# An output product moved behind those of the next two batches, its sums kept in SBUF

## The chip, the cores and the metric

One core of a Trainium2 chip runs the whole program. The metric is the device time of one execution in microseconds, the median of several runs. The engines are TensorE (PE, with PEld for its weight loads), VectorE (DVE), ScalarE (ACT), GpSimd (POOL) and SyncE (SP); SyncE's queue issues every DMA of this kernel.

## The reference

Attention with a causal mask and a bias, then two feed-forward parts, for 4 batches of 576 tokens, 512 channels. The change lies between the last lines of the first part and the first of the second:

```python
# first part (x is the attention's output)
h = gelu(x @ w_in);  u, v = halves of h
gated = u * (einsum('ts,bsd->btd', w_sg, norm(v) * g_ln) + b_sg)
x2 = x + gated @ w_out
# second part (x is x2)
theta = x2 @ w_theta
y = einsum(w_tok_r, x2 * cos(theta)) + einsum(w_tok_i, x2 * sin(theta))
u = x2 + y
out = u + max(u @ w_ch, 0)
```

## The kernel before

All values are fp32. A matrix product is made of three: each operand is split into a high half (rounded, on ScalarE) and a low half (the rest, on VectorE or GpSimd), and high x high, high x low and low x high are summed in PSUM. Activations lie transposed, channels in the partitions, in four strips (dt or ft) of 128 channels by 576 tokens; a strip is multiplied in two halves of 288 tokens (HALF).

The attention, lines 419 to 452, runs for all batches with the first part of the earlier batches as fill. Behind it stands the last batch's first part, and with it what the change touches, in run (lines 850 to 896):

- ffn_in and ffn_gate of batch 3. ffn_gate (lines 649 to 672) writes the gated strips of every batch to memory (gd, line 672). x, the attention's output, is in memory too (xd).
- The second part's weights: second_weights (lines 914 to 934) is a generator, prep, that loads 64-bit words (wraw), and in split64 (lines 455 to 472) makes fp32 of them in three VectorE instructions (wta, lines 466, 467 and 469) and the two halves, the low one on GpSimd (wol, wtl, wkl, wcl). Such a unit is called a weight group below. Each step of the output product pulls one (self.later).
- wout (lines 675 to 700) is the output product of one batch. It loads four gated strips (gr), splits them (gh on ScalarE, gl on VectorE, line 90), and for each of four strips dt loads x (xr, line 689), multiplies 2 x 12 matmuls (wo), adds x on VectorE (line 697) and writes x2 to memory (x2d, line 699).
- theta (lines 703 to 766) is the start of the second part of one batch. It loads the batch's x2 in one transfer (x2T, line 708), splits it (x2s, with a small copy xt on GpSimd), and for each of five token tiles makes a transposition (tp), a product (th, 12 matmuls) and a chain over ScalarE and VectorE (kk, an, sn, cs) to cos and sin, and two products zf of them with x2.
- mix (lines 778 to 814) multiplies the split zf (zh, zl) with the token weights (yo, 27 matmuls for each of eight outputs), then with w_ch (co), and writes the result.

The order of wout and theta is set in run: batches 0 and 1 as fill of ffn_gate(3), batch 2 alone, batch 3 as fill of theta(0), then mix(0) with theta(1) as fill, and so on. wout of batch 0 writes x2 to memory and theta(0) reads it back. From what is written there, tile's scheduler makes each engine's own order by priorities and a timeline of its own, so a step that is moved in the code moves others too. Each engine works through its list in order and waits where an operand or a buffer is not there.

PSUM tiles are shared by tags of two banks each: yo, ex, fo, tp. wraw and xr have three buffers, gr two, gh and gl six, x2T two.

Of the kernel before, what the change touches and what calls it, by code (L numbers as in the profile page):

```python
# [9 lines left out]
F32 = mybir.dt.float32  # L10
# [8 lines left out]
B, H, S, D = 4, 8, 576, 64  # L19
DM, DFF = 512, 1024  # L20
FH = DFF // 2
P = 128
# [27 lines left out]
class Kernel:  # L50
# [621 lines left out]
            nc.sync.dma_start(self.gd[b, ft], uT[:, ft])  # L672


    def wout(self, b, pool):
        nc = self.nc
        gs = []
        for ft in range(4):
            gr = pool.tile([P, S], F32, name="gr", tag="gr")
            nc.sync.dma_start(gr, self.gd[b, ft])  # L680
            gh = pool.tile([P, S], F32R, name="gh", tag="gh", bufs=6)
            gl = pool.tile([P, S], F32R, name="gl", tag="gl", bufs=6)
            self.rnd("act", gh, gr)
            self.sub("dve", gl, gr, gh)
            gs.append((gh, gl))
        for dt in range(4):
            ds = slice(dt * P, (dt + 1) * P)
            xr = pool.tile([P, S], F32, name="xr", tag="xr", bufs=3)
            nc.sync.dma_start(xr, self.xd[b, dt])
            for a, m in HALF:  # L690
                o = self.psB.tile([P, 512], F32, name="wo", tag=self.wtag)
                for ft in range(4):
                    gh, gl = gs[ft]
                    self.mm(o[:, 0:m], self.woh[:, ft, ds], gh[:, a:a + m], ft == 0, False)
                    self.mm(o[:, 0:m], self.wol[:, ft, ds], gh[:, a:a + m], False, False)
                    self.mm(o[:, 0:m], self.woh[:, ft, ds], gl[:, a:a + m], False, ft == 3)
                nc.vector.tensor_tensor(xr[:, a:a + m], o[:, 0:m], xr[:, a:a + m], op=ALU.add)  # L697
                if a:
                    nc.sync.dma_start(self.x2d[b, dt], xr)
                yield 1480.0  # L700


    def theta(self, b):

        nc = self.nc
        x2T = self.p1.tile([P, 4, S], F32, name="x2T", tag="x2T", bufs=2)
        self.x2T[b] = x2T
        nc.sync.dma_start(x2T, self.x2d[b].rearrange("t p s -> p t s"))
        xs = []
        for dt in range(4):  # L710
            x = self.p1.tile([P, 2, S], F32R, name="x2s", tag="hl", bufs=4)
# [105 lines left out]
    def run(self):  # L817
        nc = self.nc
        with ExitStack() as root, ExitStack() as right2, ExitStack() as left2:
# [40 lines left out]
            with ExitStack() as ws:  # L860
                self.stg = self.pool(ws, "stg", side="right")
                for n, _ in enumerate(self.ffn_in(B - 1)):
                    if n % 8 == 0:
                        self.later(prep)
                f3s.close()
                wq = self.pool(ws, "wq", bufs=2, side="right")

                def wo(bs):
                    for b in bs:
                        for c in self.wout(b, wq):  # L870
                            self.later(prep)
                            yield c

                self.ftags = ("yo", "ex")
                self.fill, self.ratio = wo((0, 1)), 0.8
                for c in self.ffn_gate(B - 1):
                    self.pace(c)
                left.close()
                self.wc = self.pool(left2, "wc")
                self.p1 = self.pool(left2, "p1")  # L880
                self.drain()
                self.wtag = "ex"
                for _ in wo((2,)):
                    pass
                self.fill, self.ratio = wo((3,)), 0.5
                for c in self.theta(0):
                    self.pace(c)
                self.drain()
                for _ in prep:
                    pass  # L890
# [86 lines left out]
```

## Time and profile before

| | |
|---|---|
| median of 3 runs | 708.98 us (708.6 to 710.29) |
| the profiled execution | 710.52 us |
| its span, first to last instruction | 708.7 us |
| mean granted clock of TensorE | 0.981 of full |
| TensorE matmuls (PE) busy | 662.4 us, 93% |
| VectorE (DVE) busy | 455.4 us, 64% |
| ScalarE (ACT) busy | 371.7 us, 52% |
| GpSimd (POOL) busy | 261.3 us, 37% |
| read from and written to memory | 60.38 and 19.10 MB |

In the span the attention fills some 363 us, the first part of batch 3 the time to about 416 us, the output products with the first theta the time to 507 us, and the mixing of the four batches the rest. A matmul's recorded duration is longer than the distance to the next one, because matmuls overlap; the distance is what counts, and idle time in brackets names what ended it. The granted clock is a share of 2.4 GHz; 0.5 is the lower level.

### The profile page before, as it was taken

To read this page: it belongs to the slowest core of one execution; us is meant where nothing else is said; L and a number is where in the kernel's file an instruction comes from. 1 tells how busy PE (TensorE), PEld (TensorE's weight loads), DVE (VectorE), ACT (ScalarE), POOL (GpSimd) and SP (SyncE) were. 2 spreads that over 40 slices of the span, in tenths; PEclk is the share of its full clock that TensorE was granted. 3 is DMA by queue.
4 is the path that set the end of the run, shared out by engine and by line. 5 is a ranking of instruction groups with operands and counts; after the bars stand their busy time and mean duration, and the time that the engine had idled before them with its cause. 6 is when DMAs were issued, how large, how long until landed. Compare 5 with 4: busy or idle time off the path is not lost.

```text
span 708.7 us, 12076 instructions
## 1 busy us (share of the span) xinstructions
PE 662.4 (93%) x4288; PEld 580.9 (82%) x4288; DVE 455.4 (64%) x902; ACT 371.7 (52%) x856; POOL 261.3 (37%) x273
## 2 busy tenths in 40 slices
PE   6899789799999999999999769998999999999998
PEld 4667557588879788897879669887999989989997
DVE  5566687766438544484449998898976368368522
ACT  3566656677367743786427534673753255156100
POOL 6556564458426554375237653423000100010000
PEclk9899989999999999999999989999999999999999
DMA  4646666624423354321143778972000300300101
GB/s 131 188 142 193 203 196 182 183 78 147 125 83 109 102 154 142 103 84 44 68 143 104 243 240 297 328 255 85 34 1 25 110 1 1 134 1 1 68 1 68
DMA packets 52972, 85.02 MB, mean 120 GB/s; under 512 B 9968, under 2 KB 19600, under 8 KB 52912
## 3 DMA queue, kind: packets, MB, share of 16 engines
q1 hardware_dynamic: 52912, 84.25, 38.3%
q8 instruction: 34, 0.56, 0.3%
q14 instruction: 26, 0.21, 0.1%
HBM read 60.38 MB, written 19.10 MB: 112 GB/s over the span
## 4 chain that ended last, share of the span: by engine, by line
PE 49%; DVE 7%; DMA 4%; ACT 3%; issue 2%; POOL 0%; SPq 0%; DVEq 0%; ACTq 0%
PE yo L93 16%; PE co L93 7%; PE fo L93 7%; PE th L93 6%; PE Y L93 3%; PE wo L93 3%; PE sc L93 3%; PE T L332 2%; DVE wta L469 1%; DVE wta L467 1%; DMA x2T<-x2d 1%; PE tp L720 1%; DVE wta L466 1%; DVE gl L90 1%; DMA wraw<-in_moe_w_ch 1%
## 5 line engine op out<-in xcount | busy, mean ns | idle before, releaser
L293 ACT ACTIVATE E<-sc,negm 128x448 f32<-128x448 f32 (+4 forms) x160 | 87.0, 551 | 51.4 <-DVE negm L292 50.3
L292 DVE TENSOR_REDUCE negm<-sc 128x1 f32<-128x448 f32 (+4 forms) x160 | 73.6, 481 | 43.4 <-PE sc L93 42.2
L93 PE MATMUL yo<-wkh,zl 128*128 128x288 f32 x288 | 85.3, 297 | 0.0
L93 PE MATMUL yo<-wkh,zh 128*128 128x288 f32 x288 | 85.2, 296 | 0.0
L93 PE MATMUL yo<-wkl,zh 128*128 128x288 f32 x288 | 85.1, 296 | 0.0
L332 PE MATMUL T<-ident,E 128*128 128x128 f32 x400 | 73.4, 298 | 5.0 <-ACT E L293 3.4
L93 PE MATMUL sc<-kA,qA 128*128 128x128 f32 (+2 forms) x192 | 64.9, 359 | 9.5 <-ACT E L293 7.8
L332 PEld LDWEIGHTS T<-ident,E 128*128 128x128 f32 x400 | 58.2, 194 | 17.2 <-issue 5.7
L93 PE MATMUL sc<-kB,qB 68*128 68x128 f32 (+3 forms) x192 | 61.6, 331 | 3.4 <-DMA qB<-cpos 1.8
L93 PE MATMUL fo<-x,wih 128*128 128x288 f32 x256 | 58.4, 306 | 1.5 <-ACT vT L607 0.8
L86 POOL TENSOR_SCALAR xt<-x2s 128x128 fp32r<-128x128 f32 x16 | 9.9, 634 | 134.2 <-DVE x2s L90 134.2
L93 PEld LDWEIGHTS yo<-wkh,zh 128*128 128x128 f32 x288 | 54.1, 188 | 0.3
L93 PEld LDWEIGHTS yo<-wkl,zh 128*128 128x128 f32 x288 | 54.1, 188 | 0.2
L93 PEld LDWEIGHTS yo<-wkh,zl 128*128 128x128 f32 x288 | 53.9, 188 | 0.2
L93 PE MATMUL co<-u,wch 128*128 128x288 f32 x256 | 53.1, 295 | 0.0
L93 PEld LDWEIGHTS sc<-kA,qA 128*128 128x128 f32 x192 | 38.6, 209 | 16.3 <-ACT E L293 8.4
L90 POOL TENSOR_TENSOR kB<-K,kA 64x576 fp32r<-64x576 f32 x32 | 46.6, 1456 | 10.5 <-ACT kA L82 9.1
L93 PE MATMUL wo<-gh,woh 128*128 128x288 f32 x128 | 40.4, 319 | 9.1 <-DVE xr L697 6.4
L86 POOL TENSOR_SCALAR qA<-Q 128x576 fp32r<-128x576 f32 x32 | 22.6, 705 | 69.7 <-PE sc L93 29.9
L90 POOL TENSOR_TENSOR qA<-Q,qA 64x576 fp32r<-64x576 f32 x32 | 46.3, 1446 | 2.6
L93 PE MATMUL Y<-Ef,vr 128*64 128x512 f32 (+3 forms) x256 | 47.0, 444 | 0.0
L93 PEld LDWEIGHTS fo<-x,wih 128*128 128x128 f32 x256 | 43.3, 192 | 3.9 <-issue 1.2
(169 smaller groups left out, 1878.5 us busy)
## 6 DMA issues: line engine op xcount, KB each, us to landing
Q<-in_q SPq DMA_DIRECT2D x64, 144.0 KB
K<-in_k SPq DMA_DIRECT2D x64, 144.0 KB
qB<-qA SPq DMA_DIRECT2D x32, 144.0 KB
xT<-rd SPq DMA_DIRECT2D x32, 144.0 KB
xd<-xT SPq DMA_DIRECT2D x16, 288.0 KB
gd<-uT SPq DMA_DIRECT2D x16, 288.0 KB
gr<-gd SPq DMA_DIRECT2D x16, 288.0 KB
xr<-xd SPq DMA_DIRECT2D x16, 288.0 KB
```

Of the source, the lines that this page charges most:

```text
L86: nc.gpsimd.tensor_scalar(out, src, 1.0, 1.0, op0=ALU.mult, op1=ALU.mult)
L90: e.tensor_tensor(out, a, f32(hi), op=ALU.subtract)
L93: self.nc.tensor.matmul(out, lhsT, rhs, start=start, stop=stop)
L292: nc.vector.tensor_reduce(negm[:, c:c + 1], o, axis=ax, op=ALU.max, negate=True)
L293: nc.scalar.activation(out, o, AF.Exp, bias=negm[:, c:c + 1], accum_out=sm[:, j * 5 + c:j * 5 + c + 1])
L332: nc.tensor.transpose(T[:, col:col + P], e, self.ident)
L466: nc.vector.tensor_scalar(ta.bitcast(U32), ta.bitcast(U32), 3, None, op0=ALU.logical_shift_left)
L467: nc.vector.scalar_tensor_tensor(ta.bitcast(U32), Hi, 0x80000000, ta.bitcast(U32), op0=ALU.bitwise_and, op1=ALU.bitwise_or)
L469: nc.vector.scalar_tensor_tensor(ta.bitcast(U32), L, 29, ta.bitcast(U32), op0=ALU.logical_shift_right, op1=ALU.bitwise_or)
L720: nc.tensor.transpose(tp[0:r, dt * P:(dt + 1) * P], x2T[:, dt, a:a + r], self.ident)
```

## The change

wout gets an argument kept. With it, x is loaded straight into the batch's x2T tile (a strip dt of it in place of xr), the sums are made there, and nothing is written to memory. x2_tile makes such a tile; theta makes and loads one only where the batch has none. In run, the fill of ffn_gate(3) is wout of batches 1 and 2 in place of 0 and 1; batch 0's, with kept, stands alone behind them, where batch 2's stood; batch 3's is the fill of theta(0) as before.

```diff
--- before.py
+++ after.py
@@ -672,7 +672,8 @@
             nc.sync.dma_start(self.gd[b, ft], uT[:, ft])
 
 
-    def wout(self, b, pool):
+    def wout(self, b, pool, kept=False):
+
         nc = self.nc
         gs = []
         for ft in range(4):
@@ -685,7 +686,7 @@
             gs.append((gh, gl))
         for dt in range(4):
             ds = slice(dt * P, (dt + 1) * P)
-            xr = pool.tile([P, S], F32, name="xr", tag="xr", bufs=3)
+            xr = self.x2T[b][:, dt] if kept else pool.tile([P, S], F32, name="xr", tag="xr", bufs=3)
             nc.sync.dma_start(xr, self.xd[b, dt])
             for a, m in HALF:
                 o = self.psB.tile([P, 512], F32, name="wo", tag=self.wtag)
@@ -695,17 +696,21 @@
                     self.mm(o[:, 0:m], self.wol[:, ft, ds], gh[:, a:a + m], False, False)
                     self.mm(o[:, 0:m], self.woh[:, ft, ds], gl[:, a:a + m], False, ft == 3)
                 nc.vector.tensor_tensor(xr[:, a:a + m], o[:, 0:m], xr[:, a:a + m], op=ALU.add)
-                if a:
+                if a and not kept:
                     nc.sync.dma_start(self.x2d[b, dt], xr)
                 yield 1480.0
 
 
+    def x2_tile(self):
+        return self.p1.tile([P, 4, S], F32, name="x2T", tag="x2T", bufs=2)
+
     def theta(self, b):
 
         nc = self.nc
-        x2T = self.p1.tile([P, 4, S], F32, name="x2T", tag="x2T", bufs=2)
-        self.x2T[b] = x2T
-        nc.sync.dma_start(x2T, self.x2d[b].rearrange("t p s -> p t s"))
+        if b not in self.x2T:
+            self.x2T[b] = self.x2_tile()
+            nc.sync.dma_start(self.x2T[b], self.x2d[b].rearrange("t p s -> p t s"))
+        x2T = self.x2T[b]
         xs = []
         for dt in range(4):
             x = self.p1.tile([P, 2, S], F32R, name="x2s", tag="hl", bufs=4)
@@ -867,12 +872,12 @@
 
                 def wo(bs):
                     for b in bs:
-                        for c in self.wout(b, wq):
+                        for c in self.wout(b, wq, b in self.x2T):
                             self.later(prep)
                             yield c
 
                 self.ftags = ("yo", "ex")
-                self.fill, self.ratio = wo((0, 1)), 0.8
+                self.fill, self.ratio = wo((1, 2)), 0.8
                 for c in self.ffn_gate(B - 1):
                     self.pace(c)
                 left.close()
@@ -880,7 +885,8 @@
                 self.p1 = self.pool(left2, "p1")
                 self.drain()
                 self.wtag = "ex"
-                for _ in wo((2,)):
+                self.x2T[0] = self.x2_tile()
+                for _ in wo((0,)):
                     pass
                 self.fill, self.ratio = wo((3,)), 0.5
                 for c in self.theta(0):
```

How it moves the lists of the engines, at three places. The number behind a name tells one tile from another.

SyncE, the issues around 424 to 434 us of the trace of before. gr and xr belong to output products, xd and gd are x and the gated strips in memory, wraw are raw weights. Before:

```order
L689 DMA xr_4859<-xd_57 128x576
L699 DMA x2d_58<-xr_4683 128x576
L909 DMA wraw_4918<-in_moe2_w_tok_i 128x576
L909 DMA wraw_4985<-in_moe2_w_tok_i 128x576
L699 DMA x2d_58<-xr_4771 128x576
L689 DMA xr_4969<-xd_57 128x576
L909 DMA wraw_5009<-in_moe2_w_tok_r 128x576
L680 DMA gr_5169<-gd_59 128x576
L689 DMA xr_5018<-xd_57 128x576
L699 DMA x2d_58<-xr_4859 128x576
```

and with the change:

```order
L690 DMA xr_4859<-xd_57 128x576
L690 DMA x2T_5169<-xd_57 128x576
L700 DMA x2d_58<-xr_4683 128x576
L915 DMA wraw_4918<-in_moe2_w_tok_i 128x576
L915 DMA wraw_4985<-in_moe2_w_tok_i 128x576
L690 DMA x2T_5169<-xd_57 128x576 x3
L700 DMA x2d_58<-xr_4771 128x576
L915 DMA wraw_5009<-in_moe2_w_tok_r 128x576
L690 DMA xr_4969<-xd_57 128x576
L681 DMA gr_5170<-gd_59 128x576
```

The four loads of batch 0's x, into x2T_5169, stand ahead of the write of x2d from xr_4683, and of three loads (wraw_5009, xr_4969 and the next gr). In the order before, no such load stands here.

VectorE, the start of theta of batch 0. x2s are its split halves, wta weight groups, an and kk the chain to cos and sin; gl_5190 is the last strip of batch 2 before, and gl_5401 the first of batch 3 in the change. Before:

```order
L90 TENSOR_TENSOR x2s_5397<-x2T_5380,x2s_5397 128x576
L90 TENSOR_TENSOR gl_5190<-gr_5187,gh_5189 128x576
L466 TENSOR_SCALAR wta_5108<-wta_5108 128x288
L466 TENSOR_SCALAR wta_5134<-wta_5134 128x288
L467 SCALAR_TENSOR_TENSOR wta_5108<-wraw_5107,wta_5108 128x288
L467 SCALAR_TENSOR_TENSOR wta_5134<-wraw_5133,wta_5134 128x288
L469 SCALAR_TENSOR_TENSOR wta_5108<-wraw_5107,wta_5108 128x288
L466 TENSOR_SCALAR wta_5161<-wta_5161 128x256
L469 SCALAR_TENSOR_TENSOR wta_5134<-wraw_5133,wta_5134 128x288
L467 SCALAR_TENSOR_TENSOR wta_5161<-wraw_5160,wta_5161 128x256
L90 TENSOR_TENSOR gl_5410<-gr_5407,gh_5409 128x576
L469 SCALAR_TENSOR_TENSOR wta_5161<-wraw_5160,wta_5161 128x256
```

and with the change:

```order
L698 TENSOR_TENSOR x2T_5169<-wo_5195,x2T_5169 128x288
L698 TENSOR_TENSOR x2T_5169<-wo_5218,x2T_5169 128x288
L469 SCALAR_TENSOR_TENSOR wta_5108<-wraw_5107,wta_5108 128x288
L467 SCALAR_TENSOR_TENSOR wta_5134<-wraw_5133,wta_5134 128x288
L466 TENSOR_SCALAR wta_5161<-wta_5161 128x256
L90 TENSOR_TENSOR x2s_5373<-x2T_5169,x2s_5373 128x576
L469 SCALAR_TENSOR_TENSOR wta_5134<-wraw_5133,wta_5134 128x288
L467 SCALAR_TENSOR_TENSOR wta_5161<-wraw_5160,wta_5161 128x256
L698 TENSOR_TENSOR x2T_5169<-wo_5242,x2T_5169 128x288
L90 TENSOR_TENSOR gl_5401<-gr_5398,gh_5400 128x576
L469 SCALAR_TENSOR_TENSOR wta_5161<-wraw_5160,wta_5161 128x256
L698 TENSOR_TENSOR x2T_5169<-wo_5265,x2T_5169 128x288
```

Before, the four x2s stand together (x2s_5397 is the last), and kk follows the weight groups wta_5108 to wta_5161. With the change the sums into x2T_5169 alternate with weight groups, and each x2s follows the two sums of its strip; seven more weight groups stand between this piece and the first kk.

TensorE, the same place: wo are matmuls of the output product, tp the transpositions, th the theta product. Before:

```order
L93 MATMUL wo_5143<-gl_4966,woh_4170 128x288
L720 MATMUL tp_5402<-ident_149,x2T_5380 128x128 x4
L720 MATMUL tp_5493<-ident_149,x2T_5380 128x128 x4
L93 MATMUL wo_5195<-gh_5183,woh_4170 128x288
L93 MATMUL wo_5195<-gh_5183,wol_4171 128x288
L93 MATMUL wo_5218<-gh_5183,woh_4170 128x288
L93 MATMUL wo_5218<-gh_5183,wol_4171 128x288
L93 MATMUL wo_5195<-gl_5184,woh_4170 128x288
L93 MATMUL wo_5218<-gl_5184,woh_4170 128x288
L93 MATMUL th_5449<-wth_4172,x2s_5382 128x512
L93 MATMUL th_5449<-wtl_4173,x2s_5382 128x512
```

and with the change:

```order
L93 MATMUL wo_5265<-gh_5190,wol_4171 128x288
L93 MATMUL wo_5265<-gl_5191,woh_4170 128x288
L93 MATMUL th_5440<-wth_4172,x2s_5373 128x512
L93 MATMUL th_5440<-wtl_4173,x2s_5373 128x512
L93 MATMUL th_5491<-wth_4172,x2s_5373 128x512
L93 MATMUL th_5491<-wtl_4173,x2s_5373 128x512
L93 MATMUL th_5440<-wth_4172,x2s_5373 128x512
L93 MATMUL th_5491<-wth_4172,x2s_5373 128x512
L93 MATMUL wo_5289<-gh_5172,woh_4170 128x288
L93 MATMUL wo_5289<-gh_5172,wol_4171 128x288
```

Before, the transpositions of a whole token tile stand together, and th_5449 follows with all its strips, between matmuls of batch 2's first two output tiles. With the change theta goes strip by strip in two token tiles at once (th_5440 and th_5491), each strip behind 24 matmuls of batch 0's output product.

## Rows read from the trace of the kernel before

**Rows 1.** Busy time by stretch, core 0: us, engines with instructions, PEclk, DMA share, GB/s

```profile
418.00:426.00 8.00, 6.14 (x25) 6.14 (x26) 6.70 (x13) 2.19 (x5) 3.00 (x4) 0.57 0.78 259
426.00:436.00 10.00, 9.59 (x72) 9.36 (x71) 8.58 (x21) 4.55 (x10) 3.22 (x4) 1.00 0.80 259
432.00:451.00 19.00, 17.55 (x128) 16.60 (x127) 16.86 (x35) 10.13 (x22) 6.27 (x8) 1.00 0.96 328
451.00:470.00 19.00, 19.00 (x111) 16.79 (x110) 16.82 (x38) 12.12 (x24) 6.90 (x7) 1.00 0.94 323
...
507.30:530.00 22.70, 22.70 (x168) 22.12 (x167) 18.51 (x34) 12.03 (x23) 0.00 (x0) 1.00 0.00 1
486.00:492.00 6.00, 5.58 (x31) 5.57 (x32) 3.89 (x10) 3.82 (x7) 0.73 (x1) 0.72 0.31 98
```

**Rows 2.** What TensorE waited for, 432 to 510 us: total us, times, longest us

```profile
PE wo L93 <- DVE xr L697: 2.2, 4, 1.3
PE th L93 <- DVE x2s L90: 1.2, 2, 0.9
PE th L93 <- DVE xr L697: 0.7, 1, 0.7
```

**Rows 3.** TensorE in order of time: start us, us, count, idle before

```profile
419.86 0.61 PE L93 MATMUL wo<-gh,woh 128*128 128x288 f32 x1 [4.24 <-DVE xr L697]
...
479.87 0.47 PE L93 MATMUL th<-wth,x2s 128*128 128x512 f32 x1
...
482.12 0.39 PE L93 MATMUL th<-wtl,x2s 128*128 128x512 f32 x1
...
484.66 0.50 PE L93 MATMUL th<-wth,x2s 128*128 128x512 f32 x1 [0.94 <-DVE x2s L90]
486.42 0.40 PE L93 MATMUL wo<-gh,woh 128*128 128x288 f32 x1 [1.26 <-DVE xr L697]
```

**Rows 4.** The chain that ended last, 430 to 508 us: start us, us, what

```profile
429.89 1.21 PE wo L93 x9
...
432.62 3.83 DMA gr<-gd
...
440.07 7.89 DMA x2T<-x2d
...
504.20 0.44 PE tp L720 x4
504.64 2.77 PE th L93 x12
```

**Rows 5.** VectorE's groups by line, 432 to 492 us: count, busy us, mean ns, idle

```profile
L697 DVE TENSOR_TENSOR xr<-wo,xr 128x288 f32<-128x288 f32 x21 | 9.1, 450 | 2.1 <-PE wo L93 2.0
L469 DVE SCALAR_TENSOR_TENSOR wta<-wraw,wta 128x288 uint32<-128x288 uint32 (+1 forms) x16 | 8.0, 502 | 0.1
L90 DVE TENSOR_TENSOR gl<-gr,gh 128x576 fp32r<-128x576 f32 x10 | 7.8, 776 | 2.1 <-ACT gh L82 2.0
L467 DVE SCALAR_TENSOR_TENSOR wta<-wraw,wta 128x288 uint32<-128x288 uint32 (+1 forms) x16 | 7.1, 446 | 0.1
L90 DVE TENSOR_TENSOR x2s<-x2T,x2s 128x576 fp32r<-128x576 f32 x8 | 6.5, 840 | 0.0
L466 DVE TENSOR_SCALAR wta<-wta 128x288 uint32<-128x288 uint32 (+1 forms) x16 | 5.6, 357 | 0.5 <-ACT wta L465 0.5
...
L759 DVE TENSOR_TENSOR zf<-x,cs 128x512 f32<-128x512 f32 x4 | 2.8, 710 | 0.1
```

**Rows 6.** VectorE in order of time, at 450 and at 480 us

```profile
450.77 1.42 DVE L90 TENSOR_TENSOR x2s<-x2T,x2s 128x576 fp32r<-128x576 f32 x2
...
480.65 2.05 DVE L90 TENSOR_TENSOR x2s<-x2T,x2s 128x576 fp32r<-128x576 f32 x2
```

**Rows 7.** GpSimd in order of time, at 480 us

```profile
480.85 2.44 POOL L90 TENSOR_TENSOR wcl<-wta,wch 128x256 fp32r<-128x256 f32 x2
```

**Rows 8.** ScalarE in order of time, at 490 us

```profile
490.79 0.58 ACT L745 COPY sn<-th 64x512 f32<-64x512 f32 x1 [1.42 <-DVE zf L759]
```

## The prediction

> **What bounds the kernel now.** I read the busy times by stretch first, then the waits of TensorE, and last the rows around each wait. The change neither adds nor removes a matmul, and TensorE is busy all through the stretches around it [rows 1]. So the end moves only by what TensorE idles, or works at the lower clock. The change touches the stretch from about 420 us, behind the last gate product, to 507 us, where the mixing of the first batch begins. There the reader is to see two things. Once the mixing runs TensorE has no gap (22.70 of 22.70 us from 507 us, [rows 1]), so a microsecond saved before it is one saved at the end. And between 432 and 470 us the other resources are nearly full too: the DMA engines are at 0.96 and 0.94, VectorE is busy 16.9 of 19 and 16.8 of 19 us [rows 1].
>
> What TensorE loses after 432 us is small. Matmuls of the output product waited 2.2 us for sums (xr) of VectorE, those of theta 1.2 us for split halves (x2s) and 0.7 us for a sum [rows 2]: 4.1 us. At 479.87 to 482.12 us eight theta matmuls start 0.32 us apart in place of the 0.23 us of the chain (12 in 2.77 us) [rows 3, 4]: 0.7 us. And from 486 to 492 us the granted clock is 0.72 on average [rows 1], which costs 6 x 0.28 = 1.7 us; it fell to the lower level (1.2 GHz) after TensorE had waited 0.94 and 1.26 us within 4 us [rows 3]. Together **6.5 us**, the most that the change can win. A longer wait, before 419.86 us (4.24 us, [rows 3]), lies ahead of the first row that the change moves on TensorE and VectorE; I leave it as it is.
>
> **The change, part by part.** *Removed:* four writes of x2d and one load of x2T of 1152 KB for batch 0, so 2.3 MB less traffic, 7 us at the 328 GB/s of the stretch [rows 1]. The load took 7.89 us and is in the chain [rows 4]. But it costs TensorE little: while it was under way TensorE had 17.55 busy us in 19 [rows 1], with output products of the third batch. In its own loss the load has at most the 0.7 us wait of theta and some of the 2.2 us. The transfer is no gain by itself; what counts is which engine is late next. SyncE issues 9 - 4 = 5 transfers fewer.
>
> *Not removed:* batch 1 takes the place of batch 0. Its x2T of 1152 KB is loaded at the same place in SyncE's queue, behind the third gr of what is now batch 0, and the fourth gr is queued behind it. The DMA engines thus stay full until about 450 us. Nobody needs that x2T before theta of batch 1, near 485 us, so its own landing is covered by 40 us.
>
> *Moved forward:* the four loads of x for batch 0 (now into x2T) stand ahead of x2d, wraw, xr and gr that were next. That is 4 x 288 KB, 3.5 us at 328 GB/s; the DMA engines have a 0.2 share free in 426 to 436 us [rows 1], 2 us, so some 1.5 us of it reaches the transfers behind. They are free to start: the tile lies where the gate's operands were, and TensorE had ended the gate 4.24 us before 419.86 us [rows 3]. First to feel it is gr of the next batch: issued at 432.62 us, it took 3.83 us and stands in the chain [rows 4]. In the new order VectorE has to do both gl of that batch before the sum of strip xr_5018, where it did one before; TensorE waits for that sum, and the matmuls of wo_5195 wait for the same gl. Bounds: 0 (the weight groups between cover it) and 3.5 us (all of it reaches TensorE). Then wo_5242 can only start when the sums of wo_5195 are taken, behind the last gl. I take 1.5 us and 0.5 us, nearest to the 2.2 + 0.7 us that the same sums cost now: **2.0 us** lost in 432 to 451 us.
>
> *Theta of batch 0 starts strip by strip.* For each of four strips TensorE now does 24 output matmuls at 0.134 us (9 in 1.21 us, [rows 4]), two transposes at 0.11 us (4 in 0.44) and 6 theta matmuls at 0.23 us: 3.2 + 0.2 + 1.4 = 4.8 us. VectorE does in the same time two sums at 0.45 us, one x2s at 0.84, one gl at 0.78 and two to three weight groups of 0.36 + 0.45 + 0.50 = 1.3 us [rows 5]: 5.1 to 6.4 us by those durations, but an instruction starts before the last ends (two x2s took 1.42 us at 450.77 us, [rows 6]), some 0.1 us each, so 4.2 to 5.3 us. It has up to 2 us in hand, because x2s is asked for only after the next strip's first twelve matmuls. Over three strips it falls behind by 0 to 1.5 us, more where GpSimd gets in its way. So TensorE waits 0 to 1.1 us for the last x2s; I take **0.5 us** in 451 to 470 us. All ten weight groups still to do are then behind VectorE, which is why theta's chain (kk, an, zf) runs after them without them in between.
>
> *Before the first mixing.* Theta of batch 1 needs its four x2s; they now stand between zf and an of batch 0's last tiles, as before, but without weight groups and their GpSimd halves beside them. Before, this place cost 0.94 + 1.26 us [rows 3], the 1.7 us of clock and some of the 0.7 us. In its place comes a wait for a transpose bank: the third set of transposes of batch 1 needs the bank, so the copy, of the first (tp has two banks), and ScalarE does that copy only behind its copy into sn for the last theta tile, which waits for the last zf. Behind the fourth x2s VectorE has a sum and two zf (0.45 + 2 x 0.71, [rows 5]) and then ScalarE two copies of 0.58 us [rows 8], 3.0 us less 0.2 for overlap; TensorE has four to six matmuls and a set of transposes there, 1.8 us: 1.0 us left. GpSimd's four xt copies still collide with x2s, and add up to 1 us. Bounds 0 and 4.1 us (0.94 + 1.26 + 1.7, with 0.2 of the theta matmuls). I take **1.6 us**, and no fall of the clock, since no two waits of a microsecond stand together.
>
> *Beside the first mixing.* Two tiles of theta of batch 1 move behind the first mixing product. Each is 12 matmuls, which TensorE does either way. VectorE gets 2 x 6 instructions like zf (0.71 us, [rows 5]) more there, some 8 us; it has 22.7 - 18.5 = 4.2 us free in 507 to 530 us [rows 1]. I cost it at **0**; were that cover gone, TensorE would wait for a theta bank, 1 us at most.
>
> *Sum:* new losses 2.0 + 0.5 + 1.6 = 4.1 us in place of 6.5 us, a gain of 2.4 us. The profiled execution took 710.52 us (708.7 of span), so 708.1; the median of the runs is 708.98 us, 1.5 us below that execution, and I forecast against it: **706.6 us**.
>
> **The rivals.** *A. VectorE doesn't keep up with the packed weight groups; no gain.* Ten groups stand now between the first sum into x2T and the first kk, where before they were spread up to 487 us. Each group ends in a GpSimd subtraction, and beside such a one VectorE's instructions stretch: two x2s took 2.05 us beside two wcl, against 1.42 us at 450.77 us [rows 6, 7]. At up to 0.6 us each, eight such collisions are 4.8 us, less the 2 us in hand: 2.8 us more loss than I count, so 6.9 in place of 6.5 us, **709.4 us**. For it speaks the sum of VectorE, 16.8 of 19 us; against it that the order of now pays for such collisions too, at 480 to 486 us, where they cost most. The Trainium skill, "SBUF — State Buffer", section "Who interferes with whom", says that a VectorE instruction with two SBUF inputs and a GpSimd instruction that reads SBUF take one shared port in turn, and whichever comes second blocks until the first is done. By that rule the packed groups would cost this rival's time; the trace agrees that both took longer side by side [rows 6, 7].
>
> *B. One long wait at 438 to 450 us; slower.* The four loads ahead delay gr and xr of the next batch so far that both output tiles in work stand still at once. It decides where TensorE idles about 4 us at a piece: after the 4.24 us wait the clock was 0.57 on average from 418 to 426 us [rows 1, 3], a loss of 0.43 x 8 = 3.4 us. Price 4.2 + 3.4 = 7.6 in place of the 2.0 us counted, so 5.6 us more: **712.2 us**. For it speaks the full DMA; against it that SyncE issues gr at the same time as before, since a VectorE release sets it, and that 2 us of the 3.5 are free.
>
> *C. The stall goes with the traffic; a larger gain.* With 2.3 MB less, gr and wraw land sooner than in the 3.83 us of now and only the bank wait stays: 1.0 us lost in place of 6.5, **703.5 us**. Against it: batch 1's x2T fills the same place.
>
> That the change does not take the traffic away is excluded by the order: no x2d and no x2T load of that batch is issued.
>
> **How the numbers follow.** A measurement of this kernel can tell some 0.3%, 2.1 us, from no change. My forecast (705 to 706.9 us) has 0.38, C 0.08, A with all between 706.9 and 711.1 us 0.34, B 0.20. Faster 0.46, same 0.34, slower 0.20. The range leaves out the upper half of B and half of C's chance and more: 703.6 to 711.8 us. It takes in the bounds 0 + 0 + 1.0 us of new losses (703.5, nearly) and 3.5 + 1.1 + 4.1 us (711.2).
>
> **What would show it.** Right: no x2d/x2T transfer for batch 0; in the waits of TensorE from 432 us on theta's wait for x2s and the output product's wait for xr together near 3 us; granted clock 1.0 from 480 to 492 us; the first mixing matmul near 499 us (504.64 + 2.77 = 507.41 [rows 4], less 6.0 us for two theta tiles that now follow it, less 2.4). Wrong: a clock below 1.0 anywhere between 432 and 500 us; a wait over 2 us at the output product that waits for xr_5018 (B) or at the first theta tile (A); a wait of the mixing products for zl; or a loss of the same size in the first mixing.

## The result, and the profile after

The changed kernel takes 712.69 us (median of 22 runs, 709.95 to 717.15) beside 708.94 us of the kernel before (22 runs): 1.0077 of it, with a 95% interval from 1.006 to 1.0094. It is slower; the forecast was 706.6 us. Run again later beside other kernels it gave 1.0077 once more (1.0047 to 1.0107). The ratio is the one on record; it is not the quotient of the two medians, which is 1.0053 (3.75 us), and where the two ways of comparing tell different things below, both are given.

The end moves by what happens behind the gate. The wait of 4.24 us for the last sum ahead of it [rows 3] stands in both traces (4.23 us in the changed one); from the matmul behind it to the end of the span the kernel before takes 708.7 - 419.86 = 288.8 us, the changed one 709.6 - 417.45 = 292.2 us, 3.3 us more. In the second traces of both, taken later, it is 286.4 and 289.8 us, 3.4 us more. The waits of TensorE in 430 to 510 us of the changed kernel, which answer to [rows 2]:

```profile
engine line waited for: us in total, times, longest us
PE wo L93 <- DVE xr L698: 3.0, 2, 2.5
PE tp L725 <- ACT x L728: 2.5, 1, 2.5
PE wo L93 <- DVE gl L90: 1.4, 1, 1.4
PE wo L93 <- DVE x2T L698: 0.8, 1, 0.8
```

Theta no longer waits for x2s or for a sum. In their place stand one wait at an output product of the third batch, two near 450 us and one at the transpositions. The single matmuls, from TensorE's timeline:

```profile
417.45 0.61 PE L93 MATMUL wo<-gh,woh 128*128 128x288 f32 x1 [4.23 <-DVE xr L698]
...
435.15 0.40 PE L93 MATMUL wo<-gh,woh 128*128 128x288 f32 x1 [2.54 <-DVE xr L698]
...
450.01 0.40 PE L93 MATMUL wo<-gl,woh 128*128 128x288 f32 x1 [1.40 <-DVE gl L90]
...
452.35 0.40 PE L93 MATMUL wo<-gh,woh 128*128 128x288 f32 x1 [0.77 <-DVE x2T L698]
...
496.90 0.67 PE L725 MATMUL tp<-ident,x2T 128*128 128x128 f32 x4 [2.53 <-ACT x L728]
```

The same stretches by windows (us; busy time of PE, PEld, DVE, ACT, POOL; granted clock, DMA share, GB/s), to be read beside [rows 1]:

```profile
432.00:434.00 2.00, 0.62 (x5) 0.39 (x3) 0.57 (x2) 0.89 (x3) 1.26 (x2) 1.00 1.04 408
434.00:436.00 2.00, 0.84 (x6) 0.85 (x7) 1.56 (x5) 0.97 (x2) 0.28 (x1) 0.99 1.04 404
436.00:438.00 2.00, 2.00 (x10) 2.00 (x9) 1.34 (x3) 1.49 (x4) 0.81 (x1) 0.50 1.06 411
438.00:440.00 2.00, 2.00 (x13) 2.00 (x12) 1.97 (x7) 0.90 (x3) 0.00 (x0) 0.65 1.02 394
...
453.00:492.00 39.00, 38.55 (x251) 35.34 (x250) 35.38 (x72) 24.84 (x48) 12.42 (x16) 1.00 0.38 125
...
496.00:498.00 2.00, 1.10 (x6) 1.00 (x7) 1.28 (x2) 1.98 (x5) 0.00 (x0) 0.85 0.00 0
498.00:500.00 2.00, 2.00 (x7) 1.52 (x6) 2.00 (x5) 2.00 (x5) 0.00 (x0) 0.50 0.03 8
500.00:502.00 2.00, 2.00 (x10) 1.64 (x9) 2.00 (x4) 1.54 (x3) 0.00 (x0) 0.79 0.00 0
502.00:525.00 23.00, 23.00 (x157) 21.67 (x156) 19.10 (x36) 13.85 (x24) 0.00 (x0) 1.00 0.00 1
```

Behind each wait of 2.5 us the clock is at its lower level (0.50, 1.2 GHz): 2 x 0.50 + 2 x 0.35 = 1.7 us lost from 436 us, and 2 x (0.15 + 0.50 + 0.21) = 1.7 us from 496 us. The strip by strip stretch between them, 453 to 492 us, loses 0.45 us in 39, and beside the mixing TensorE is full. So the changed kernel loses 2.54 + 1.7 + 1.40 + 0.77 + 0.45 + 2.53 + 1.7 = 11.1 us where the kernel before lost 6.5. That is 4.6 us more, and the tail is 3.3 us longer; the other 1.3 us these rows do not account for.

**Where the first wait comes from.** SyncE's timeline (the first of the four x2T loads is issued at 422.04 us), then ScalarE's, then VectorE's:

```profile
425.26 1.48 SPq L690 DMA_DIRECT2D x2T<-xd  x3
426.84 0.38 SPq L700 DMA_DIRECT2D x2d<-xr  x1
427.69 0.33 SPq L915 DMA_DIRECT2D wraw<-in_moe_w_tok_r  x1
...
437.49 0.43 SPq L712 DMA_DIRECT2D x2T<-x2d  x1
...
440.35 0.54 SPq L690 DMA_DIRECT2D xr<-xd  x1
```

```profile
432.23 0.80 ACT L82 CAST wkh<-wta 128x288 fp32r<-128x288 f32 x2 [2.10 <-DVE wta L469]
433.91 0.46 ACT L465 ACTIVATE wta<-wraw 128x288 f32<-128x288 f32 x1 [0.88 <-DMA wraw<-in_moe_w_tok_r]
...
495.66 0.58 ACT L750 COPY sn<-th 64x512 f32<-64x512 f32 x1 [1.41 <-DVE zf L764]
496.26 0.59 ACT L728 COPY x<-tp 128x512 f32<-128x512 f32 x1
```

```profile
434.41 0.31 DVE L466 TENSOR_SCALAR wta<-wta 128x288 uint32<-128x288 uint32 x1 [1.84 <-ACT wta L465]
434.64 0.82 DVE L698 TENSOR_TENSOR xr<-wo,xr 128x288 f32<-128x288 f32 x2
...
448.84 0.46 DVE L698 TENSOR_TENSOR xr<-wo,xr 128x288 f32<-128x288 f32 x1 [3.44 <-DMA xr<-xd]
449.21 0.75 DVE L90 TENSOR_TENSOR gl<-gr,gh 128x576 fp32r<-128x576 f32 x1
...
450.24 0.75 DVE L90 TENSOR_TENSOR gl<-gr,gh 128x576 fp32r<-128x576 f32 x1
```

The load of one weight tile (wraw) is issued at 427.69 us, behind loads of the kept batch's x into x2T. It lands about 433.9 us. ScalarE and VectorE, which take their lists in order, reach that weight group first; the two sums that TensorE waits for stand behind it and run only at 434.64 us. (The Trainium skill, "TensorE: Matmul & The Clock Gate", section "Architectural detail: the array is 16× 32×32, not 1× 128×128", says that the queues of VectorE and ScalarE are strictly first in, first out; these rows agree, 1.84 us at VectorE.)

Not all of the 2.54 us is the load's. The kernel before has a load of the same weights; its rows, ScalarE's and TensorE's:

```profile
433.99 0.48 ACT L465 ACTIVATE wta<-wraw 128x288 f32<-128x288 f32 x1 [0.89 <-DMA wraw<-in_moe_w_tok_r]
434.83 0.43 ACT L82 CAST wkh<-wta 128x288 fp32r<-128x288 f32 x1 [0.36 <-DVE wta L469]
...
436.01 0.40 PE L93 MATMUL wo<-gh,woh 128*128 128x288 f32 x1 [0.42 <-DVE xr L697]
```

There the load was issued at 430.73 us and used 3.3 us later; here it takes 6.2 us, so it is slower with the four loads ahead. But ScalarE waited for it there too (0.89 us, and 2.19 us when that kernel was run again), and TensorE only 0.42 us (0.92 us). In the changed kernel the lists differ as well: two wkh, which wait 2.10 us for VectorE, now stand ahead of this conversion on ScalarE, so that it could not have begun before 433.03 us. By these rows the late load alone is worth at most 0.88 of the 2.54 us, and the rest, some 0.4 us of which stood there before too, lies in the order of the lists; no run changes one without the other.

The waits at 450 us are of the same kind: xr, issued at 440.35 us behind the 1152 KB load of batch 1's x2T, holds up a sum for 3.44 us, and both gl stand behind that sum. That this load is what makes xr late is not shown (x2T of batch 1 later, below).

**The last wait.** ScalarE's copy into sn waits 1.41 us for the zf that still reads sn, and the copy of x that frees the transposition bank stands behind it.

**The DMA.** The whole program moves 82.66 MB, the kernel before 85.02. But in the 27 us that decide (425 to 452 us here, 427.4 to 454.4 us before, as the changed execution is 2.4 us ahead), the changed one moves more, not less; first the kernel before, then the changed one, from the DMA view:

```profile
DMA packets 4272, 8.78 MB, mean 325 GB/s; under 512 B 456, under 2 KB 456, under 8 KB 4270
```

```profile
DMA packets 4421, 9.08 MB, mean 336 GB/s; under 512 B 475, under 2 KB 475, under 8 KB 4419
```

### The profile page after: what moved, and what is told of

It reads as the page before. It is cut to its first block, busy times and chain, and to the rows that moved or that the text cites. A ratio compares the mean times of both kernels' runs of the same rounds, so it can differ in the third digit from the quotient of the medians.

```text
span 709.6 us, 12054 instructions
## 1 busy us (share of the span) xinstructions
PE 663.7 (94%) x4288; PEld 583.1 (82%) x4288; DVE 455.1 (64%) x902; ACT 373.2 (53%) x856; POOL 258.6 (36%) x273
## 2 busy tenths in 40 slices
DMA packets 51868, 82.66 MB, mean 116 GB/s; under 512 B 9888, under 2 KB 19520, under 8 KB 51808
## 4 chain that ended last, share of the span: by engine, by line
PE 46%; DVE 9%; ACT 4%; DMA 4%; issue 2%; POOL 1%; SPq 0%; DVEq 0%; ACTq 0%
PE yo L93 16%; PE co L93 7%; PE fo L93 7%; PE th L93 5%; PE Y L93 3%; PE sc L93 3%; PE T L332 2%; DVE wta L467 2%; PE wo L93 2%; DVE wta L469 1%; DMA xr<-xd 1%; DMA wraw<-in_moe_w_out 1%; DVE gl L90 1%; DVE wta L466 1%; DMA gr<-gd 1%
## 5 line engine op out<-in xcount | busy, mean ns | idle before, releaser
L86 POOL TENSOR_SCALAR xt<-x2s 128x128 fp32r<-128x128 f32 x16 | 8.4, 532 | 144.1 <-DVE x2s L90 144.1
```

Of the source, the lines that this page charges most:

```text
L86: nc.gpsimd.tensor_scalar(out, src, 1.0, 1.0, op0=ALU.mult, op1=ALU.mult)
```

## The experiments

My theory after this reading: two separate causes, loads issued ahead of a weight load that VectorE's list then waits for (theory 1), and the copy into sn ahead of the copy that frees the bank (theory 2). Ratios below are to the kernel before run beside, with their 95% intervals. A kept sum is a sum into batch 0's kept x2T tile.

### First round: one cause at a time

**x in xr.** x of the kept batch goes through the rotating xr tiles.

```diff
-            xr = self.x2T[b][:, dt] if kept else pool.tile([P, S], F32, name="xr", tag="xr", bufs=3)
+            xr = pool.tile([P, S], F32, name="xr", tag="xr", bufs=3)
+            to = self.x2T[b][:, dt] if kept else xr
...
-                nc.vector.tensor_tensor(xr[:, a:a + m], o[:, 0:m], xr[:, a:a + m], op=ALU.add)
+                nc.vector.tensor_tensor(to[:, a:a + m], o[:, 0:m], xr[:, a:a + m], op=ALU.add)
```

> Batch 0's x is loaded into the three rotating xr tiles, as all other batches' x, and only the sum is written into the kept x2T. So its loads wait for a free tile and can no longer be issued ahead of the weights, x and g of the batch before. Theory 1 (the four loads ahead hold up the weight load, VectorE waits for it in front of a sum, TensorE stops 2.54 us and then runs at half clock): the output product's waits for sums between 428 and 440 us come to less than 1 us, the granted clock stays at 1.0 from 436 to 440 us, and the time falls by 2.5 to 4.5 us against the changed kernel, to 708 to 710 us. Rival (the bytes fill the DMA engines, whatever their order): the same bytes are loaded, so the wait only moves, and the time stays within 1 us of the changed kernel, 711.5 to 713.5 us. By both the wait for the transposition bank near 497 us stays.

713.62 us, 1.007 (1.0043 to 1.0097): no gain. The wait at 435 us is gone (0.42 us in its place), but one of 1.95 us with half clock behind it stands at the first kept sum. VectorE's and TensorE's timelines there:

```profile
447.88 0.52 DVE L466 TENSOR_SCALAR wta<-wta 128x288 uint32<-128x288 uint32 x2
448.32 0.81 DVE L467 SCALAR_TENSOR_TENSOR wta<-wraw,wta 128x288 uint32<-128x288 uint32 x2
...
449.63 0.45 DVE L469 SCALAR_TENSOR_TENSOR wta<-wraw,wta 128x288 uint32<-128x288 uint32 x1
450.00 0.81 DVE L699 TENSOR_TENSOR x2T<-wo,xr 128x288 f32<-128x288 f32 x2
```

```profile
450.49 0.40 PE L93 MATMUL wo<-gh,woh 128*128 128x288 f32 x1 [1.95 <-DVE x2T L699]
```

The wait for the bank is there too, 2.85 us at 499.13 us. From 447.88 us VectorE works through seven instructions of weight groups while the two sums wait behind them. The total fits the rival, but its reason (bytes) isn't what the rows show: the place in the list moved, and the loss with it.

**Copy in kk.** For the last tile of every theta.

```diff
-                nc.scalar.copy(sn[0:64], o[64:128])
-                nc.vector.tensor_tensor(an[0:64], o[0:64], sn[0:64], op=ALU.add)
+                nc.scalar.copy(k[0:64], o[64:128])
+                nc.vector.tensor_tensor(an[0:64], o[0:64], k[0:64], op=ALU.add)
```

> The changed kernel, where the upper half of theta's last tile is copied into kk, which is free earlier, in place of sn, which VectorE still reads for zf. Theory 2 (ScalarE's copy into sn waits for VectorE's zf and holds up the copy that frees the transposition bank): the wait of the transposes near 497 us (2.53 us) and the half clock behind it (1.7 us) go, the time falls by 3 to 4.5 us against the changed kernel, to 708 to 710 us. Rival (VectorE is behind at that place, and whatever TensorE needs next is late too): a wait for x2s or for a sum of over 1.5 us takes its place and the time falls by less than 1.5 us, 711 to 713 us.

710.71 us, 1.0035 (1.001 to 1.0059). No transposition waits any more; 2 us less by the medians, less than theory 2 expected and more than its rival. Waits of 0.6 us for an, in the next theta, are new.

**x2T of batch 1 later.**

```diff
+            with self.tc.issue_after(self.last.ins):
-            nc.sync.dma_start(self.x2T[b], self.x2d[b].rearrange("t p s -> p t s"))
+                nc.sync.dma_start(self.x2T[b], self.x2d[b].rearrange("t p s -> p t s"))
```

(self.last is the last gr load issued so far.)

> The changed kernel, but the 1152 KB load of batch 1's x2T is issued behind the last gr of the fourth batch, some 15 us later. Theory 3 (that load stands ahead of an xr load of the kept order and of gr, and makes them late, 8.37 us for one xr): the waits for gl and for a sum at 450 and 452 us (1.40 and 0.77 us) go, the wait at 435 us stays, the time falls by 1 to 2.5 us, to 710 to 711.7 us. Rival (VectorE's packed weight groups make those sums late): they stay, and the time is within 0.8 us of the changed kernel.

716.87 us, 1.0118 (1.0089 to 1.0146): 4 us slower than the changed kernel, which neither expected. With that load gone from its place the other lists shift, and now ScalarE is stuck; its timeline:

```profile
448.74 0.47 ACT L465 ACTIVATE wta<-wraw 128x288 f32<-128x288 f32 x1 [1.74 <-DMA wraw<-in_moe_w_tok_i]
449.99 0.47 ACT L465 ACTIVATE wta<-wraw 128x288 f32<-128x288 f32 x1 [0.79 <-DMA wraw<-in_moe_w_tok_i]
450.36 0.66 ACT L82 CAST gh<-gr 128x576 fp32r<-128x576 f32 x1
```

gh stands behind two weight groups that wait for their loads; TensorE then waits 0.30, 1.07, 0.54 and 1.31 us for gh, gl and a sum between 451 and 457 us, and the clock is at 0.50 from 456 to 460 us. The wait at 435 us stays (2.97 us). Theory 3, that the 1152 KB load costs the time, falls as stated; since the lists moved too, the run does not show what the load costs.

**Both** (x in xr, copy in kk).

> The edits of the two runs with x in xr and the copy in kk together. If theories 1 and 2 both hold, the losses add up: 6 to 8 us less than the changed kernel, 705 to 707 us, and below the kernel before by 2 to 4 us. If a wait that is removed is paid at the next place (VectorE full): less than 4 us against the changed kernel, 708.5 us or more, not below the kernel before.

710.26 us, 1.0033 (1.0012 to 1.0054): 2.4 us below the changed kernel, as the second line of the expectation has it. The 1.95 us wait of the run with x in xr is there too.

### Second round: the loads' place, and the weight groups

**Loads late.** x goes straight into x2T, but behind the third batch's x; with the copy in kk.

```diff
+            if kept:
+                with self.tc.issue_after(self.lx.ins):
+                    nc.sync.dma_start(xr, self.xd[b, dt])
+            else:
-            nc.sync.dma_start(xr, self.xd[b, dt])
+                self.lx = nc.sync.dma_start(xr, self.xd[b, dt])
```

> The copy in kk, and the four loads of batch 0's x go into the kept x2T as in the changed kernel but are issued behind the last xr load of the third batch. Theory 1 (loads ahead hold up a weight load, VectorE's list is then stuck): the wait of 2.5 us near 435 us goes, and as fewer weight groups stand ahead of the first x2T sum than with x in xr (three instructions, not seven), the wait there is under 1 us and the clock stays at 1.0 from 436 to 460 us: 706.5 to 708.5 us, 2 to 4 us below the copy in kk alone. Rival (430 to 455 us carries more transfers than the DMA engines do in that time, so that some load is always late, whichever): a wait of 1.5 us or more with half clock behind it stays between 430 and 460 us, and the time is 709.5 to 711.5 us.

708.63 us, 1.0025 (1.0005 to 1.0046): just above what theory 1 forecast, and by the ratio only 0.1% below the copy in kk alone (1.0035). The wait at 435 us is 0.42 us, but a wait of 1.80 us with half clock stays at the first kept sum, as the rival said. Again a weight group stands ahead of the sum and waits 0.86 us for its load.

**Spread.** Both edits of the first round, and every weight group pulled in wout must stand behind the sum before it.

```diff
+                            with self.tc.issue_after(self.sum.ins):
-                            self.later(prep)
+                                self.later(prep)
```

> Both edits (x in xr, copy in kk), and each weight group pulled in the output product may stand in VectorE's list only behind the sum before which it was pulled: the groups are spread and some of them move beside theta's kk, an and zf. Rival A of the prediction (packed weight groups ahead of the sums make TensorE wait, 1.95 us at 450 us and half clock behind it): that wait falls under 0.8 us, the granted clock stays at 1.0 from 450 to 460 us, 707 to 709 us. Other theory (VectorE has as much to do before the first mixing whatever the order): the groups delay kk, an and zf in place of the sums, a new wait of TensorE for a theta or transposition bank appears after 470 us, and the time is 710 us or more.

710.11 us, 1.0032 (1.0008 to 1.0055). The clock is 1.00 from 410 us to the mixing, and the last wait of the gate's stretch, 4.23 us with half clock behind it in the changed kernel, is 2.06 us without. But there are more short waits (1.34 and 1.32 us for sums at 432.75 and 447.95 us, theta for an 2.3 us in three from 470 us on, the first mixing 1.0 us for zl): as the other theory said, groups moved out of one place are in the way in another. What was gained at the gate is lost again; that it could be had without the loss was not tried.

**The kernel before with the copy in kk.**

> The kernel before with the copy in kk alone. Theory 2 (the bank wait came with the change): no transposition waits for that bank in the kernel before, so its time changes by less than 1 us, 707.9 to 709.5 us. Rival (the copy into sn costs the kernel before as much): 2 us less, about 706.5 us, and then the gain of the copy in kk says nothing of the change.

710.47 us, 1.0041 (1.0018 to 1.0064): slower, which neither expected. So the copy in kk for all four thetas has a price of its own.

**Both, and x2d written.** Batch 0's sums are written to x2d too (the condition `if a and not kept` becomes `if a`).

> Both edits (x in xr, copy in kk), and batch 0's sums are also written to x2d as before the change, where nobody reads them: 1152 KB of writes more between 450 and 470 us. The step of the prediction that the removed traffic is no gain by itself: within 0.8 us of both edits alone. Rival C (less traffic is the gain): at least 1.5 us slower than both edits alone, since the loads of g and of the weights behind the writes land later.

709.65 us, 1.0031 (1.0008 to 1.0054), beside 1.0033 without the writes: the writes removed (1152 KB) are worth nothing that shows in the time. The trace is less plain: TensorE's waits in 430 to 500 us come to 6.8 us with the writes and 4.4 us without, but with the writes the 1.7 us of half clock did not come in that execution. The load of 1152 KB that the change also removed was not put back.

### Third round: the copy in the first theta alone, and pinned weight groups

**Pinned.** Loads late, the copy in kk if b == 0 only, and:

```diff
-                        for c in self.wout(b, wq, b in self.x2T):
-                            self.later(prep)
+                        for n, c in enumerate(self.wout(b, wq, b in self.x2T)):
+                            if b == 0:
+                                with self.tc.issue_after(self.sum.ins):
+                                    self.later(prep)
+                            elif b != 2 or n < 5:
+                                self.later(prep)
```

(self.sum is the last sum added so far.)

> As the run with the x loads behind the third batch's (loads late, copy in kk for the first theta alone), and the last weight groups (from the 33rd of 42) are pulled beside the kept batch and may stand in VectorE's list only behind the sum before them. Theory 1 in its general form (a weight group that waits for its load, ahead of a sum in VectorE's list, is what makes TensorE wait, wherever it falls): the wait of 1.80 us for the first x2T sum near 450 us falls under 0.5 us, the granted clock stays at 1.0 from 450 to 460 us, and the time is 1.5 to 3.5 us below the same kernel without the pinning, 705 to 707 us, below the kernel before. Rival (the sum itself is late, since g and x land late): the wait stays over 1.2 us, time within 1 us of the kernel without pinning.

708.72 us, 0.9991 (0.9962 to 1.0019). **The same without pinning:**

> The x loads of the kept batch behind the last xr load of the third batch, and the copy in kk for the first theta alone. If the copy in kk costs 0.9 us in the three later thetas, as the stretch from the first mixing product to the end shows in the profiles (208.6 to 208.8 us with it, 207.9 without): 0.5 to 1.2 us below the run with the copy in all four, 707.4 to 708.2 us. Rival (that stretch differs by chance from execution to execution): no difference, 708.6 us.

708.14 us, 0.9988 (0.9963 to 1.0013). The two edits take the whole loss away, but no gain over the kernel before is shown. The pinning gains nothing (0.9991 beside 0.9988), as its rival said of the time, where theory 1 expected 1.5 to 3.5 us. **The kernel before with the copy in the first theta alone:**

> The kernel before, with the copy in kk for the first theta alone. If the 2.5 us that the copy in kk cost the kernel before came from the three later thetas: 708 us, as the kernel before. If it came from the first theta (another order of output product and theta ahead of the first mixing): 710 us or more.

709.9 us, 0.9997 (0.9975 to 1.002): in the kernel before, the price of the copy in kk lies in the three later thetas. What it is made of there was not followed, and the changed kernel does not show it: 1.0035 with the copy in all four, 1.0029 in the first alone (fourth round). **The kernel before unchanged:**

> The kernel before once more, with nothing changed, as a measure of how well two equal programs agree: 0.998 to 1.002 of it, 707 to 709.5 us. If equal programs differ by more than 0.3%, differences of 2 us between the variants say nothing.

709.04 us, 0.9998 (0.9974 to 1.0021). Two equal programs agree. Its trace has the waits of [rows 2] again, but not the half clock near 486 us [rows 1]:

```profile
484.00:488.00 4.00, 1.97 (x12) 1.67 (x13) 3.96 (x9) 1.18 (x3) 1.56 (x3) 1.00 0.10 37
488.00:492.00 4.00, 4.00 (x33) 4.00 (x33) 2.77 (x6) 2.54 (x6) 0.74 (x1) 1.00 0.31 116
```

### Fourth round: each edit alone, beside the changed kernel

> The changed kernel once more, unchanged, beside the three others: 0.5 to 0.9% slower than the kernel before, with waits of about 2.5 us near 435 us and near 497 us. If one of the two waits is missing in this execution, it comes and goes by chance and can't carry the loss.

712.44 us, 1.0077 (1.0047 to 1.0107), and both waits are there again, with half clock behind the first, none behind the second:

```profile
436.20 0.61 PE L93 MATMUL wo<-gh,woh 128*128 128x288 f32 x1 [2.69 <-DVE xr L698]
...
497.61 0.66 PE L725 MATMUL tp<-ident,x2T 128*128 128x128 f32 x4 [2.23 <-ACT x L728]
```

> The changed kernel with one edit: the four loads of the kept batch's x are issued behind the last xr load of the third batch. Theory 1 (the loads ahead cause the 2.54 us wait and the half clock behind it): this alone is worth 2 to 4 us against the changed kernel run beside it, and the wait for the transposition bank near 497 us stays. Rival (only the copy in kk is worth something; the loads' place is not): within 1 us of the changed kernel.

711.68 us, 1.0036 (1.0003 to 1.0069). The wait at 435 us is 0.42 us. One of 2.17 us stands at the first kept sum, and what the copy into sn holds up here is not the transposition but the mixing (1.34 us for zh, 0.62 for zl), with half clock behind the first kept sum and again behind these two.

> The changed kernel with one edit: in the first theta alone the upper half of the last tile is copied into kk in place of sn. Theory 2: worth 2 to 4 us against the changed kernel run beside it, the wait near 497 us is gone, the wait of 2.5 us near 435 us stays. Rival (the loads' place is all): within 1 us of it.

710.48 us, 1.0029 (1.0004 to 1.0054). The wait near 497 us is gone, that at 437 us is 2.58 us, with half clock behind it and again from 454 us, behind waits of 1.32 and 0.77 us.

By the ratios the loads' place is worth 0.41% and the copy 0.48%; together 0.89%, and the kernel with both came to 0.9988, which is 0.89% below 1.0077. The single figures have an uncertainty of about 0.4% each; that they add up is shown no better than that. By the medians of this round the copy is worth 2.0 us and the loads' place 0.8 us, which would be the rival's; and the tail behind the gate is 292.1 us with the loads late, 289.9 with the copy, 292.2 and 289.8 in the two traces of the changed kernel, 287.2 with both edits. So what the loads' place is worth alone stays open. What the traces do show is that each wait goes with its edit: near 435 us it is 2.54 to 2.97 us in all five with the loads ahead and 0.42 to 1.34 us in the eight with them later, and a transposition waits over 2 us for its bank only where the copy goes into sn.

> Loads late, copy in kk in the first theta, last weight groups behind the sums of the kept batch, once more for its trace. Theory 1 in its general form: the wait for the first x2T sum near 450 us is under 0.5 us and no half clock stands between 430 and 500 us; 0.5 to 2 us below the kernel before. Rival: a wait of over 1 us stays there, or comes back at theta's banks; not below the kernel before.

706.95 us, 0.9982 (0.9955 to 1.0009), the lowest of all, yet shown neither below the kernel before nor below the kernel without pinning. VectorE's timeline, and two waits of TensorE:

```profile
449.05 0.46 DVE L702 TENSOR_TENSOR x2T<-wo,x2T 128x288 f32<-128x288 f32 x1 [0.49 <-PE wo L93]
449.42 0.30 DVE L466 TENSOR_SCALAR wta<-wta 128x288 uint32<-128x288 uint32 x1
449.64 0.45 DVE L702 TENSOR_TENSOR x2T<-wo,x2T 128x288 f32<-128x288 f32 x1
451.14 0.31 DVE L466 TENSOR_SCALAR wta<-wta 128x288 uint32<-128x288 uint32 x1 [1.05 <-ACT wta L465]
```

```profile
449.56 0.40 PE L93 MATMUL wo<-gh,woh 128*128 128x288 f32 x1 [0.42 <-DVE x2T L702]
...
471.83 0.50 PE L93 MATMUL th<-wth,x2s 128*128 128x512 f32 x1 [1.97 <-DVE an L760]
```

The weight group still waits 1.05 us, for a conversion that waits for its load, but now behind the first two kept sums, and TensorE's wait is 0.42 us in place of 1.09 in the same kernel without pinning; the clock is 1.00 from 430 to 500 us in both. Most of it comes back as 1.97 us in place of 1.39 at a theta bank: TensorE's waits in 430 to 500 us come to 4.1 us with the pinning and 4.3 us without.

## Why the prediction was wrong, point by point

- **The most that can be won, 6.5 us:** the trace of the unchanged kernel run again has waits of 3.0 us for xr, 1.2 for x2s and 0.7 for theta's sum, 4.9 us beside the 4.1 counted, but not the 1.7 us of half clock. That comes and goes behind the same two waits (0.94 and 1.26 us), and should have stood as a chance, not as a term.
- **The removed traffic is no gain by itself:** right as far as it was tried; with the writes put back the time did not change (1.0031 beside 1.0033). The removed load was not tried.
- **The loads moved forward, 2.0 us in 432 to 451 us:** this is the step that failed. The prediction named x2d, wraw, xr and gr as queued behind the four loads, and then followed only gr. The trouble came by wraw. Its late landing, and the new order of ScalarE's list, stop a weight group on ScalarE and VectorE, and the sums of the third batch behind it, from 432.6 us on, ahead of the place that I looked at. The loss there was 2.54 + 1.7 + 1.40 + 0.77 = 6.4 us; the waits alone, 4.7 us, are above the upper bound of 3.5 us, because that bound counted transfer time and neither the order of the lists nor the clock. The two waits that were forecast, 1.5 and 0.5 us, came to 1.40 and 0.77 us, but the gl were late behind a sum that waited for xr and not by their own gr, so that their size is partly luck.
- **Strip by strip, 0.5 us in 451 to 470 us:** 0.45 us in 453 to 492 us. The size is right by luck: it is one wait of 0.46 us, of an output product for a sum at 473.15 us, and no wait for x2s came. VectorE's instructions did stretch beside GpSimd, as rival A has it (gl at 455.96 us took 1.26 us beside wkl, against 0.75 at 449.21 us), but no wait of TensorE stands in 453 to 470 us. The trace agrees there with the rule of the Trainium skill, "SBUF — State Buffer", section "Who interferes with whom", that the prediction names.
- **Before the first mixing, 1.6 us and no fall of the clock:** the mechanism was right (sn, then the copy for the bank), the size wrong: 2.53 us of wait in place of 1.0, and 1.7 us of clock in place of 0. "No two waits of a microsecond stand together" was a rule made from one case; one wait of 2.5 us was enough. No wait for x2s came.
- **Beside the first mixing, 0:** right, 23.00 of 23.00 us from 502 us on, as before [rows 1]. The prediction's own figures (8 us more for VectorE, 4.2 us free) spoke against it; VectorE is busy 19.10 of the 23.00 us there, hardly fuller than before (18.51 of 22.70).
- **Sum:** 11.1 us of losses in place of 4.1. Of the 7.0 us missing, 3.4 are half clock (1.7 twice), 2.7 the waits at 435 to 452 us (4.7 in place of 2.0), and 0.9 the bank wait (2.53 in place of 1.6).
- **Rivals:** B came closest in time (712.2 us) and in kind (loads ahead, then half clock), but it looked for one wait of 4 us at 438 to 450 us; it was 2.54 us from 432.6 us on, and 4.2 of the 11.1 us were at the bank. A's collisions cost nothing, but its weight groups did: not by their speed, by their place in the list. The range cut off the upper half of B, which is where the result lies.

## What to carry to other kernels

When a change lets loads start early, list what stands behind them in the DMA queue, and for each of these who waits for it in order: an unimportant load (weights for later) is the dangerous one where its consumer stands ahead of an urgent instruction in an engine's list. A free buffer is a permission to start, and a kernel whose DMA is full may want it withheld: issuing four loads some 20 us later (440 to 449 us in place of 422 to 426 us) took a wait of 2.5 us away here, while writing 1152 KB more cost nothing that shows in the time. On engines that take their lists in order, look at who else has to pass behind a waiting copy, and see what filler work stands ahead of an urgent instruction; pinning it behind, though, only moved the wait here (4.1 us of waits beside 4.3).

## What the runs showed that I had not expected

The clock fell to its lower level after single waits of 1.80 us (loads late), 1.95 us (x in xr), 2.17 and 2.5 us, and did not fall after 1.95 us (both with writes), 1.97 us (pinned, 471.83 us) and 2.23 us (the changed kernel again, 497.61 us). Nor does it take a wait of that length: in the changed kernel run again it was at 0.50 from 454 to 456 us, behind waits of 0.79 and 0.77 us at 450.24 and 452.58 us, and in the first trace it stayed at 1.00 behind 1.40 and 0.77 us at the same place. By the length of a wait alone these runs don't tell which it will be. The falls in 430 to 510 us cost about 1.7 us each, one 3.4 us (x2T of batch 1 later, from 454 us); so half clock is a chance to be priced with waits like these, not a term.
